# Sums of e over the token groups of batches 0 to 2 on VectorE in a fused cross-attention and ReGLU kernel

## The chip, the cores and the metric

One core of one Trainium2 chip. The metric is the device time of one execution in microseconds (us). The kernel before takes 224.06 us, the median of three runs (224.03 to 224.24).

## The reference

Eight batches b with eight heads; x has 512 tokens of 64 numbers per head, state has 32 rows of 64. The attention runs both ways, and its result goes through a feed-forward layer:

```
scores  = x @ state^T / 8          a  = softmax over the 32 states
xread   = a @ state
scores2 = state @ x^T / 8          a2 = softmax over the 512 tokens
sread   = a2 @ x
h       = concat([xread, sread]) over tokens, heads side by side   -> 4352 rows of 512
out     = (relu(h @ w_gate) * (h @ w_val)) @ w_out                   (512 -> 1536 -> 512)
```

scores2 is scores transposed. So one e = exp(scores) serves both directions: xread divides it by its sums over the states, sread by its sums over the tokens. The change is about the sums over the tokens.

## The kernel before, in words

The 512 tokens of a batch lie as 128 partitions by four groups c (NC = 4), the eight heads as two halves kc (NK = 2) of four heads. e of one batch is the tile e_sn: 128 partitions, kc, c, and 4 heads x 32 states = 128 columns. Four such tiles exist.

The weights are applied through state: U = state @ w (u_unit, c_unit, copied out by u_out L309 and c_out L319), and the normalised a, transposed to ANS, is multiplied with U. gv_mm (L324) makes gate and value products into two PSUM banks, relu (L351, on ACT, the ScalarE) writes g_sb, mult (L355, on DVE, the VectorE) writes h_sb. With 12 blocks of 128 columns (jf) for each batch these are the bulk of the work. The last product with w_out goes by seven block products (o_half, L419, a Strassen-like scheme): POOL (GpSimd) forms sums of h blocks (h_sums, L385 to L387; h_last, L394), and once the sums of w_out blocks (w_sum, L363). Results leave through o_c (L429, ACT copies the w bank), o_a (L435, DVE adds the z bank) and DMAs on SP.

Attention of a batch: att_sc (L186), att_exp (L190, ACT), att_sum (L196, L198, DVE), att_scale (L202, DVE, or POOL where the list says so), then transposes (att_T and att_out L222, or a DMA).

sread of a batch is sr_mm. It first multiplies x (stationary) with e into the bank sr_ps (32 matmuls at L235 for batches 0 to 2, whose x was cast while it was loaded; 16 at L240 for the others). Behind that it sums e over the tokens with sel, a matrix of ones: a matmul with sel sums over the partitions, and the four groups c accumulate in PSUM. Where held has no ("es", b), that is 2 parities x 2 halves x 4 groups = 16 matmuls of 64 columns (L255). Where it has, only 8 (L247): the four groups have been added before by sr_pre (three adds in float32, L263, on POOL), the sum is split into two bfloat16 parts, the high one by an ACT copy (L265) and the rest by a subtraction (sr_low, L271), and the matmuls go over these two parts. The sums es_f and the parts es have one buffer each. sr_norm (L277, L282) divides and writes br. br feeds the products of the sread rows at the end of the kernel.

Order. Nothing is scheduled by a planner at run time. Each engine works off its own instructions in the order in which the program gives them, and waits on semaphores of other engines. For batches 0 to 2, and part of 3 and 4, the order is a list of steps written out by hand (program, L568 to L602), where srm.0 is sr_mm(0), mu.1.8 is mult(1, 8) and so on: ga and gb are the halves kc of gv, re is relu, mu mult, oh o_half, oc and oa o_c and o_a, u and uo u_unit and u_out, sc, ex, nr and nx the attention steps, aT and ao att_T and att_out, hs and hl h_sums and h_last, ws w_sum, xc a cast of x, srm and srn sr_mm and sr_norm. From batch 3's fifth block on, a loop over batches and blocks gives the order (L635 to L660). There sr_pre and sr_low are called for batches 3 to 7 (L647, L648), with POOL. In the list they are not called: batches 0 to 2 take the 16 matmuls of L255. PSUM has six general banks (ps_r) that all products, transposes and scores share; a product waits until the bank it takes has been read out.

Of the kernel before, what the change touches and what calls it, by code (L numbers as in the profile page):

```python
# [11 lines left out]
ALU = mybir.AluOpType  # L12
# [4 lines left out]
def kernel(  # L17
# [9 lines left out]
    nc = tc.nc  # L27

    B, H, S, D = x.shape
# [48 lines left out]
    xf, xb, xT, e_sn, a_sn, ANS, U, hsb, sr_sb = {}, {}, {}, {}, {}, {}, {}, {}, {}  # L78
# [8 lines left out]
    held = {}  # L87
# [168 lines left out]
                                     e[:, kc, c, :, slot(2 * kc, parity)],  # L256
                                     start=False, stop=(parity == 1 and kc == 1 and c == NC - 1), skip_group_check=True)

    def sr_pre(b):

        t = small.tile([128, NK, 128], FP32, name="es_f", tag="es_f", bufs=1)
        for c in range(1, NC):
            nc.gpsimd.tensor_tensor(out=t, in0=t if c > 1 else e_sn[b][:, :, 0], in1=e_sn[b][:, :, c], op=ALU.add)  # L263
        es = held["es", b] = small.tile([128, 2, NK, 128], BF16, name="es", tag="es", bufs=1)
        nc.scalar.copy(out=es[:, 0], in_=t)  # L265
        held["es_f", b] = t

    def sr_low(b, eng="pool"):

# [264 lines left out]
    ws = ((moe_w_gate, wg_sb), (moe_w_val, wv_sb))  # L534
# [23 lines left out]
    def x_cast(b, i, eng):  # L558
# [5 lines left out]
             "gb": lambda b, jf: gv(b, jf, (1,)), "re": relu, "mu": mult, "oh": o_half, "oc": o_c, "oa": o_a, "os": o_s,  # L564
             "hs": h_sums, "hl": h_last, "ws": w_sum, "xd": lambda b: x_dma(b, (nc.sync,)), "xg": lambda b: x_dma(b, (nc.gpsimd,)),
             "xh": x0_cast, "xc": x_cast,
             "xt": x_trans_dma, "aD": att_aT_dma, "srp": sr_pre, "srl": sr_low, "srm": sr_mm, "srn": sr_norm}
    program = """  # L568
    stc.0.2.dve spin.7 stT.0.2 sto.0.2.1.act spin.1 xh.0.dve spin.1 xT.0.0 sto.0.2.0.dve xh.1.act xT.0.1
    xo.0.0.dve xT.0.3 xo.0.1.dve sc.0.0 spin.1 xo.0.3.dve ex.0.0 nr.0.0 nx.0.0 xT.0.2 xo.0.2.act sc.0.1 ex.0.1  # L570
# [12 lines left out]
    mu.0.11 xo.2.3.act ga.0.10 gb.0.10 sc.2.0 re.0.10 mu.0.10 hs.0.1 ga.1.10 gb.1.10 ex.2.0 re.1.10 ws.0.pool  # L583
    ga.1.11 sc.2.1 ex.2.1 u.2.1.0 gb.1.11 nr.2.0 re.1.11 oh.0.1 nx.2.0 uo.2.1.0.0.act mu.1.11 aT.2.0 mu.1.10
    c.1.4 uo.2.1.0.1.act u.2.0.0 ao.2.0.act oh.0.2 oh.0.3 co.1.4.0.dve ga.1.8 nr.2.1 xc.3.0.act ws.1.pool
    hs.0.2 oc.0.1 oh.0.4 co.1.4.1.act xc.3.1.pool uo.2.0.0.0.act nx.2.1.pool ga.1.9 xt.3 oa.0.3 oh.0.6
    ws.2.pool gb.1.8 re.1.8 gb.1.9 oh.0.5 ws.3.pool re.1.9 mu.1.8 aT.2.1 hl.0 uo.2.0.0.1.act xd.4 xc.4.0.pool
    xc.4.1.pool hs.1.0 ao.2.1.act oh.0.7 hs.1.2 ga.2.0 gb.2.0 mu.1.9 ga.2.3 gb.2.3 xt.4 hs.1.1 ga.2.1 gb.2.1
    re.2.0 oc.0.5 mu.2.0 re.2.1 ga.2.2 re.2.3 gb.2.2 re.2.2 mu.2.1 oh.0.8 xd.5 u.2.1.1024 mu.2.3 u.2.0.1024
    uo.2.0.1024.0.dve uo.2.1.1024.0.act uo.2.0.1024.1.act oh.0.9 u.2.1.512 u.2.0.512 oc.0.9 oh.0.10  # L590
    uo.2.0.512.0.act uo.2.1.512.1.act sc.3.0 uo.2.1.512.0.dve ga.2.5 oa.0.9 oh.0.12 oh.0.13 uo.2.1.1024.1.act
    ga.2.4 uo.2.0.512.1.act gb.2.4 oh.0.11 re.2.4 gb.2.5 ga.2.7 oc.0.11 oh.1.0 os.0.11 mu.2.2 ex.3.0 mu.2.4
    oa.0.13 re.2.5 sc.3.1 ga.2.6 mu.2.5 nr.3.0 gb.2.6 srm.0 nx.3.0 ex.3.1 oh.1.1 srn.0 re.2.6 gb.2.7 re.2.7
    mu.2.6 nr.3.1 ga.2.8 mu.2.7 gb.2.8 re.2.8 oh.1.2 mu.2.8 u.3.0.0 uo.3.0.0.0.act u.3.0.512 uo.3.0.512.0.act
    uo.3.0.0.1.act oh.1.3 stT.4.8 u.3.1.0 uo.3.1.0.0.act nx.3.1.pool ga.2.9 aD.3 gb.2.9 sto.4.8.0.act oc.1.1
    oa.1.3 re.2.9 mu.2.9 srm.1 srn.1 sto.4.8.1.act uo.3.0.512.1.act oh.1.4 oh.1.5 oc.1.5 ga.2.10 gb.2.10
    ga.2.11 re.2.10 gb.2.11 mu.2.10 re.2.11 mu.2.11 xc.5.0.act oh.1.6 oh.1.7 u.3.1.512 u.3.1.1024 u.3.0.1024
    oh.1.8 hs.2.0 uo.3.1.0.1.dve ga.3.0 gb.3.0 uo.3.1.512.0.act uo.3.0.1024.0.act xc.5.1.pool sc.4.0 ga.3.1
    oh.1.9 hl.1 uo.3.1.1024.1.dve hs.2.1 uo.3.1.1024.0.act uo.3.1.512.1.act hs.2.2 ex.4.0 ga.3.3 gb.3.1 re.3.0
    ga.3.2 uo.3.0.1024.1.dve re.3.1 gb.3.2 mu.3.0 oc.1.9 oa.1.9 re.3.2 gb.3.3 oh.1.10 re.3.3 xt.5 mu.3.3 srm.2  # L600
# [9 lines left out]
    def at(b, jf, f, *args):  # L610
        units.setdefault(NF * b + jf, []).append(lambda: f(*args))
# [33 lines left out]
            at(s, 3, x_dma, b + 2, (nc.sync,))  # L645
    for b in range(3, B):
        at(*((b, 5) if b < B - 1 else (b, 2)), sr_pre, b)  # L647
        at(*((b, 5) if b < B - 1 else (b, 2)), sr_low, b, "pool")  # L648
        at(*((b + 1, 0) if b < B - 1 else (b, 4)), sr, b)
    for g in range(first, NF * (B + 1)):  # L650
        b, jf = divmod(g, NF)
# [44 lines left out]
```

## Time and profile before

| what | value |
|---|---|
| median of three runs | 224.06 us |
| the profiled execution's own time | 224.17 us |
| its span in the profile | 222.1 us |
| mean granted TensorE clock | 0.997 |
| busy: PE, DVE, ACT, POOL | 213.4, 150.3, 128.7, 164.1 us |
| L255, the 16 sums matmuls of batches 0 to 2 | 48, started from 64.8 to 84.4 us |
| L263, the sums on POOL of batches 3 to 7 | 15, started from 88.9 to 175.3 us |

A row of the timeline gives start (us from the span's start), duration, engine, line, operation, what is written from what, shape, and in brackets the idle time ahead of it with what ended it. Rows of the same kind that follow each other are merged (x6). Durations of neighbours may overlap by some hundredths. PE is TensorE. A row of the stretches gives for each engine the busy us, in brackets the number of instructions started, then granted clock and DMA share.

### The profile page before, as it was taken

To read this page: it belongs to the slowest core of one execution; us is meant where nothing else is said; L and a number is where in the kernel's file an instruction comes from. 1 tells how busy PE (TensorE), PEld (TensorE's weight loads), DVE (VectorE), ACT (ScalarE), POOL (GpSimd) and SP (SyncE) were. 2 spreads that over 40 slices of the span, in tenths; PEclk is the share of its full clock that TensorE was granted. 3 is DMA by queue.
4 is the path that set the end of the run, shared out by engine and by line. 5 is a ranking of instruction groups with operands and counts; after the bars stand their busy time and mean duration, and the time that the engine had idled before them with its cause. 6 is when DMAs were issued, how large, how long until landed. Compare 5 with 4: busy or idle time off the path is not lost.

```text
span 222.1 us, 5525 instructions
## 1 busy us (share of the span) xinstructions
PE 213.4 (96%) x2214; PEld 139.3 (63%) x2214; DVE 150.3 (68%) x263; ACT 128.7 (58%) x247; POOL 164.1 (74%) x162
## 2 busy tenths in 40 slices
PE   6879999999999999999999999999999999999992
PEld 2535445565665657656765666566656666888881
DVE  3579967855486848878787778777977485343531
ACT  2468976876757883566556655656565454322231
POOL 7946199899999996699949993996299719933210
PEclk9999999999999999999999999999999999999998
DMA  6999999039195409920298037102320121021106
GB/s 160 193 196 196 193 201 282 20 62 265 31 206 201 97 0 207 243 72 3 74 233 218 3 91 191 52 0 97 83 61 0 50 97 47 3 96 47 50 27 209
DMA packets 42361, 25.32 MB, mean 114 GB/s; under 512 B 18816, under 2 KB 41856, under 8 KB 42336
## 3 DMA queue, kind: packets, MB, share of 16 engines
q1 hardware_dynamic: 29408, 17.04, 29.4%
q0 software_dynamic: 12416, 7.41, 22.1%
q10 hardware_dynamic: 512, 0.52, 0.7%
q8 instruction: 17, 0.28, 0.5%
q14 instruction: 8, 0.07, 0.1%
HBM read 18.35 MB, written 8.91 MB: 123 GB/s over the span
## 4 chain that ended last, share of the span: by engine, by line
PE 82%; POOL 7%; ACT 4%; DVE 3%; DMA 2%; issue 1%; DVEq 0%; POOLq 0%
PE gv_ps L324 34%; PE w_ps L419 17%; PE z_ps L419 12%; PE gv_ps L342 5%; PE up L299 4%; PE sc_ps L186 2%; DMA st_f<-in_state_dram 2%; POOL s L386 2%; POOL s L385 2%; POOL h_sb L387 2%; POOL h_sb L394 2%; PE zs_ps L419 1%; ACT g_sb L351 1%; PE ws_ps L419 1%; PE xT_ps L169 1%; PE upc L299 1%
## 5 line engine op out<-in xcount | busy, mean ns | idle before, releaser
L355 DVE TENSOR_TENSOR h_sb<-gv_ps,g_sb 128x512 bf16<-128x512 f32 (+1 forms) x108 | 69.1, 657 | 42.3 <-ACT g_sb L351 31.3
L324 PE MATMUL gv_ps<-ans,U 128*128 128x512 bf16 x384 | 94.9, 379 | 0.2
L351 ACT ACTIVATE g_sb<-gv_ps 128x512 bf16<-128x512 f32 (+1 forms) x108 | 61.4, 576 | 37.3 <-PE gv_ps L324 27.5
L419 PEld LDWEIGHTS <-h_sb 128*128 128x128 bf16 x510 | 49.4, 98 | 16.4 <-issue 1.7
L324 PEld LDWEIGHTS <-U 128*128 128x128 bf16 x384 | 35.7, 98 | 31.7 <-issue 1.7
L385 POOL TENSOR_TENSOR s<-h_sb 128x512 bf16<-128x512 bf16 x24 | 27.7, 1153 | 19.3 <-DVE h_sb L355 19.3
L394 POOL TENSOR_TENSOR h_sb<-h_sb,s 128x512 bf16<-128x512 bf16 x24 | 27.0, 1152 | 7.2 <-PE z_ps L419 7.2
L429 ACT COPY o_sb<-w_ps 128x512 f32<-128x512 f32 x32 | 18.8, 587 | 18.4 <-PE w_ps L419 15.8
L386 POOL TENSOR_TENSOR s<-s,h_sb 128x512 bf16<-128x512 bf16 x24 | 28.0, 1167 | 1.9
L309 ACT CAST U<-up 128x512 bf16<-128x512 f32 x43 | 22.7, 595 | 10.0 <-PE up L299 10.0
L387 POOL TENSOR_TENSOR h_sb<-h_sb 128x512 bf16<-128x512 bf16 x24 | 28.1, 1171 | 0.0
L419 PE MATMUL w_ps<-wo_sb,h_sb 128*128 128x256 bf16 x192 | 26.2, 273 | 0.0
L419 PE MATMUL z_ps<-wo_sb,h_sb 128*128 128x256 bf16 x186 | 24.1, 273 | 0.0
L419 PEld LDWEIGHTS <-s 128*128 128x128 bf16 x204 | 19.2, 98 | 7.7 <-issue 2.8
L435 DVE TENSOR_TENSOR o_sb<-z_ps,o_sb 128x512 f32<-128x512 f32 (+1 forms) x23 | 15.5, 675 | 6.8 <-ACT o_sb L429 4.2
L309 DVE CAST U<-up 128x512 bf16<-128x512 f32 x29 | 18.4, 684 | 1.6 <-PE up L299 1.6
L196 DVE TENSOR_REDUCE cs<-e_sn 128x16 f32<-128x512 bf16 x16 | 10.9, 680 | 5.4 <-ACT e_sn L190 5.4
L190 ACT ACTIVATE e_sn<-sc_ps 128x512 bf16<-128x512 f32 x16 | 9.6, 600 | 6.5 <-PE sc_ps L186 6.5
L419 PE MATMUL w_ps<-t2w,s 128*128 128x256 bf16 x96 | 13.0, 273 | 0.0
L419 PE MATMUL w_ps<-t,h_sb 128*128 128x256 bf16 x96 | 12.3, 272 | 0.1
L419 PE MATMUL z_ps<-t,s 128*128 128x256 bf16 x90 | 12.0, 273 | 0.0
L299 PEld LDWEIGHTS <-stT 64*32 64x32 bf16 x480 | 6.1, 89 | 7.1 <-issue 4.6
(86 smaller groups left out, 228.5 us busy)
## 6 DMA issues: line engine op xcount, KB each, us to landing
out_dram<-o_sb SPq DMA_DIRECT2D x31, 256.0 KB, 2.7
xf<-in_x_dram SPq DMA_DIRECT2D x4, 1024.0 KB, 6.9
wg_sb<-in_moe_w_gate_dram POOLq DMA_DIRECT2D x6, 256.0 KB, 9.4
wv_sb<-in_moe_w_val_dram POOLq DMA_DIRECT2D x6, 256.0 KB, 9.8
wo_sb<-in_moe_w_out_dram POOLq DMA_DIRECT2D x2, 768.0 KB, 15.7
xf<-in_x_dram POOLq DMA_DIRECT2D x1, 1024.0 KB, 18.8
xb<-in_x_dram POOLq DMA_DIRECT2D x3, 256.0 KB, 7.0
xb<-in_x_dram POOLq DMA_DIRECT2D x1, 512.0 KB, 11.8
```

Source lines behind the costliest of these rows:

```text
L299: nc.tensor.matmul(dst[kc][q:q + 32], stT[r:r + 64, b, j, 32 * sl:32 * sl + 32], wsb[r:r + 64, j, lo:lo + n], start=True, stop=True)
L309: copy[eng](out=U[b][:, w, kc, lo:lo + 512], in_=held["u", b, w, lo][kc])
L324: nc.tensor.matmul(ps[w], U[b][:, w, kc, f0:f0 + 128], ANS[b][:, kc].rearrange("p c t -> p (c t)"), start=(kc == 0), stop=(kc == NK - 1))
L351: nc.scalar.activation(out=g_sb[:, 0:n], in_=ps[0][:, 0:n], func=AF.Relu)
L355: nc.vector.tensor_tensor(out=dst, in0=ps[1][:, 0:n], in1=held["g", b, jf][:, 0:n], op=ALU.mult)
L385: tt(out=s_block(b, 1, i), in0=a21, in1=a22, op=ALU.add)
L386: tt(out=s_block(b, 2, i), in0=s_block(b, 1, i), in1=a11, op=ALU.subtract)
L387: tt(out=a21, in0=a11, in1=a21, op=ALU.subtract)
L394: {"dve": nc.vector, "pool": nc.gpsimd}[eng].tensor_tensor(out=a12, in0=a12, in1=s_block(b, 2, i), op=ALU.subtract)
L419: nc.tensor.matmul(ps[:, HM * c:HM * c + HM], a[:, i, 128 * c:128 * c + 128], w[:, i], start=(i == 0 and (p in ("p1", "p2", "p5") and c == ...
L429: nc.scalar.copy(out=o_sb, in_=held["acc", b, "w", 0])
L435: nc.vector.tensor_tensor(out=o_sb[:, cols], in0=banks[c if isinstance(c, int) else 0][:, cols], in1=o_sb[:, cols], op=ALU.add)
```

## The change

Batches 0 to 2 get the sums ahead of their sr_mm too, so that sr_mm takes the branch with 8 matmuls. sr_pre gets an engine to add on, and the ACT copy becomes a function of its own, sr_high. In the loop, batches 3 to 7 call the three one after the other, on POOL, ACT and POOL as before. In the list, for each of batches 0 to 2, three steps are new: srp (three adds on DVE), srh (the copy on ACT) and srl (the subtraction, on DVE).

```
-    def sr_pre(b):
+    def sr_pre(b, eng="pool"):

         t = small.tile([128, NK, 128], FP32, name="es_f", tag="es_f", bufs=1)
         for c in range(1, NC):
-            nc.gpsimd.tensor_tensor(out=t, in0=t if c > 1 else e_sn[b][:, :, 0], in1=e_sn[b][:, :, c], op=ALU.add)
+            {"dve": nc.vector, "pool": nc.gpsimd}[eng].tensor_tensor(out=t, in0=t if c > 1 else e_sn[b][:, :, 0],
+                                                                    in1=e_sn[b][:, :, c], op=ALU.add)
+        held["es_f", b] = t
+
+    def sr_high(b):
+
         es = held["es", b] = small.tile([128, 2, NK, 128], BF16, name="es", tag="es", bufs=1)
-        nc.scalar.copy(out=es[:, 0], in_=t)
-        held["es_f", b] = t
+        nc.scalar.copy(out=es[:, 0], in_=held["es_f", b])
...
     for b in range(3, B):
         at(*((b, 5) if b < B - 1 else (b, 2)), sr_pre, b)
+        at(*((b, 5) if b < B - 1 else (b, 2)), sr_high, b)
         at(*((b, 5) if b < B - 1 else (b, 2)), sr_low, b, "pool")
```

The list with the new steps (marked here by brackets, the other steps as before, left out where dots stand):

```
 ... uo.2.0.0.0.act nx.2.1.pool ga.1.9 xt.3 oa.0.3 [srp.0.dve] oh.0.6
 ws.2.pool gb.1.8 re.1.8 gb.1.9 oh.0.5 ws.3.pool re.1.9 mu.1.8 aT.2.1 hl.0 uo.2.0.0.1.act [srh.0] xd.4 xc.4.0.pool
 xc.4.1.pool hs.1.0 ao.2.1.act oh.0.7 hs.1.2 ga.2.0 gb.2.0 mu.1.9 [srl.0.dve] ga.2.3 gb.2.3 ...
 ... os.0.11 mu.2.2 [srp.1.dve] ex.3.0 mu.2.4 oa.0.13 re.2.5 sc.3.1 ga.2.6 mu.2.5 nr.3.0 gb.2.6 srm.0 nx.3.0
 ex.3.1 oh.1.1 srn.0 [srh.1] re.2.6 gb.2.7 re.2.7 mu.2.6 [srl.1.dve] nr.3.1 ga.2.8 mu.2.7 gb.2.8 re.2.8 oh.1.2
 mu.2.8 [srp.2.dve] u.3.0.0 ... oc.1.1 oa.1.3 re.2.9 mu.2.9 srm.1 srn.1 [srh.2] sto.4.8.1.act
 uo.3.0.512.1.act oh.1.4 oh.1.5 oc.1.5 ga.2.10 gb.2.10 ga.2.11 re.2.10 gb.2.11 mu.2.10 [srl.2.dve] re.2.11 mu.2.11 ...
```

More of the change, by code (lines that the diff above doesn't have):

```diff
@@ L566 @@
              "xh": x0_cast, "xc": x_cast,
-             "xt": x_trans_dma, "aD": att_aT_dma, "srp": sr_pre, "srl": sr_low, "srm": sr_mm, "srn": sr_norm}
+             "xt": x_trans_dma, "aD": att_aT_dma, "srp": sr_pre, "srh": sr_high, "srl": sr_low, "srm": sr_mm, "srn": sr_norm}
     program = """
@@ L585 @@
     c.1.4 uo.2.1.0.1.act u.2.0.0 ao.2.0.act oh.0.2 oh.0.3 co.1.4.0.dve ga.1.8 nr.2.1 xc.3.0.act ws.1.pool
-    hs.0.2 oc.0.1 oh.0.4 co.1.4.1.act xc.3.1.pool uo.2.0.0.0.act nx.2.1.pool ga.1.9 xt.3 oa.0.3 oh.0.6
-    ws.2.pool gb.1.8 re.1.8 gb.1.9 oh.0.5 ws.3.pool re.1.9 mu.1.8 aT.2.1 hl.0 uo.2.0.0.1.act xd.4 xc.4.0.pool
-    xc.4.1.pool hs.1.0 ao.2.1.act oh.0.7 hs.1.2 ga.2.0 gb.2.0 mu.1.9 ga.2.3 gb.2.3 xt.4 hs.1.1 ga.2.1 gb.2.1
+    hs.0.2 oc.0.1 oh.0.4 co.1.4.1.act xc.3.1.pool uo.2.0.0.0.act nx.2.1.pool ga.1.9 xt.3 oa.0.3 srp.0.dve oh.0.6
+    ws.2.pool gb.1.8 re.1.8 gb.1.9 oh.0.5 ws.3.pool re.1.9 mu.1.8 aT.2.1 hl.0 uo.2.0.0.1.act srh.0 xd.4 xc.4.0.pool
+    xc.4.1.pool hs.1.0 ao.2.1.act oh.0.7 hs.1.2 ga.2.0 gb.2.0 mu.1.9 srl.0.dve ga.2.3 gb.2.3 xt.4 hs.1.1 ga.2.1 gb.2.1
     re.2.0 oc.0.5 mu.2.0 re.2.1 ga.2.2 re.2.3 gb.2.2 re.2.2 mu.2.1 oh.0.8 xd.5 u.2.1.1024 mu.2.3 u.2.0.1024
@@ L591 @@
     uo.2.0.512.0.act uo.2.1.512.1.act sc.3.0 uo.2.1.512.0.dve ga.2.5 oa.0.9 oh.0.12 oh.0.13 uo.2.1.1024.1.act
-    ga.2.4 uo.2.0.512.1.act gb.2.4 oh.0.11 re.2.4 gb.2.5 ga.2.7 oc.0.11 oh.1.0 os.0.11 mu.2.2 ex.3.0 mu.2.4
-    oa.0.13 re.2.5 sc.3.1 ga.2.6 mu.2.5 nr.3.0 gb.2.6 srm.0 nx.3.0 ex.3.1 oh.1.1 srn.0 re.2.6 gb.2.7 re.2.7
-    mu.2.6 nr.3.1 ga.2.8 mu.2.7 gb.2.8 re.2.8 oh.1.2 mu.2.8 u.3.0.0 uo.3.0.0.0.act u.3.0.512 uo.3.0.512.0.act
+    ga.2.4 uo.2.0.512.1.act gb.2.4 oh.0.11 re.2.4 gb.2.5 ga.2.7 oc.0.11 oh.1.0 os.0.11 mu.2.2 srp.1.dve ex.3.0 mu.2.4
+    oa.0.13 re.2.5 sc.3.1 ga.2.6 mu.2.5 nr.3.0 gb.2.6 srm.0 nx.3.0 ex.3.1 oh.1.1 srn.0 srh.1 re.2.6 gb.2.7 re.2.7
+    mu.2.6 srl.1.dve nr.3.1 ga.2.8 mu.2.7 gb.2.8 re.2.8 oh.1.2 mu.2.8 srp.2.dve u.3.0.0 uo.3.0.0.0.act u.3.0.512 uo.3.0.512.0.act
     uo.3.0.0.1.act oh.1.3 stT.4.8 u.3.1.0 uo.3.1.0.0.act nx.3.1.pool ga.2.9 aD.3 gb.2.9 sto.4.8.0.act oc.1.1
-    oa.1.3 re.2.9 mu.2.9 srm.1 srn.1 sto.4.8.1.act uo.3.0.512.1.act oh.1.4 oh.1.5 oc.1.5 ga.2.10 gb.2.10
-    ga.2.11 re.2.10 gb.2.11 mu.2.10 re.2.11 mu.2.11 xc.5.0.act oh.1.6 oh.1.7 u.3.1.512 u.3.1.1024 u.3.0.1024
+    oa.1.3 re.2.9 mu.2.9 srm.1 srn.1 srh.2 sto.4.8.1.act uo.3.0.512.1.act oh.1.4 oh.1.5 oc.1.5 ga.2.10 gb.2.10
+    ga.2.11 re.2.10 gb.2.11 mu.2.10 srl.2.dve re.2.11 mu.2.11 xc.5.0.act oh.1.6 oh.1.7 u.3.1.512 u.3.1.1024 u.3.0.1024
     oh.1.8 hs.2.0 uo.3.1.0.1.dve ga.3.0 gb.3.0 uo.3.1.512.0.act uo.3.0.1024.0.act xc.5.1.pool sc.4.0 ga.3.1
```

## The prediction

> **What bounds the kernel now.** I read the page first (busy shares, slices, chain), then TensorE's waits, then busy time in stretches of 8 us around the change.
>
> ```profile
> PE 213.4 (96%) x2214; PEld 139.3 (63%) x2214; DVE 150.3 (68%) x263; ACT 128.7 (58%) x247; POOL 164.1 (74%) x162
> PE   6879999999999999999999999999999999999992
> POOL 7946199899999996699949993996299719933210
> PE 82%; POOL 7%; ACT 4%; DVE 3%; DMA 2%; issue 1%; DVEq 0%; POOLq 0%
> ```
> ```profile
> PE warm_ps L554 <- DVE warm L511: 1.2, 1, 1.2
> ```
> ```profile
> 44.00:52.00 8.00, 8.00 (x82) 5.54 (x80) 4.54 (x8) 5.89 (x12) 8.00 (x6) 1.00 0.57 114
> 68.00:76.00 8.00, 8.00 (x118) 5.18 (x118) 5.39 (x11) 6.82 (x15) 7.92 (x8) 1.00 0.49 143
> ```
>
> PE is busy in every slice from the fourth on, is 82% of the chain, and its longest single wait is the 1.2 us before the first matmul. So a microsecond taken off PE in the list of steps is a microsecond off the end, and a microsecond for which PE is made to wait there is one added. The two stretches are where the change acts: PE has 8.00 of 8 us. But so, nearly, has POOL (8.00 and 7.92), while DVE has 4.54 and 5.39. DVE looks like the free place for the sums. Whether it is free beside a POOL that never pauses is what decides.
>
> **What goes: 24 matmuls.**
>
> ```profile
> 51.03 3.62 PE L324 MATMUL gv_ps<-ans,U 128*128 128x512 bf16 x16
> 54.48 0.82 PE L419 MATMUL w_ps<-wo_sb,h_sb 128*128 128x256 bf16 x6
> ...
> 64.15 0.68 PE L235 MATMUL sr_ps<-e_sn,xb 128*64 128x32 bf16 x32
> 64.76 0.64 PE L255 MATMUL sr_ps<-e_sn,sel 128*128 128x64 bf16 x16
> 65.24 0.82 PE L419 MATMUL w_ps<-wo_sb,h_sb 128*128 128x256 bf16 x6
> ```
>
> From start to start the 16 matmuls of L255 take 65.24 - 64.76 = 0.48 us, 0.03 each. Each of the three batches loses 8 of them: 3 x 8 x 0.03 = **0.72 us saved**, all on the path.
>
> **What comes: 12 instructions on DVE, 3 on ACT.** No row of before has such an add on DVE. The nearest are below (L202, 512 elements, 0.69 us; two of L282, 128 elements, 0.59 together, so 0.29 each). Straight between them, 256 elements take 0.42 us; I use that, with 0.29 and 0.69 as ends. By duration alone three adds are 1.3 us a batch.
>
> The price is not the duration. These adds read both operands from SBUF, as L202 does, and DVE's other frequent product (L355) does not (one operand is in PSUM). Look at what happens when L202 meets POOL:
>
> ```profile
> 42.07 1.15 POOL L385 TENSOR_TENSOR s<-h_sb 128x512 bf16<-128x512 bf16 x1 [0.96 <-DVE h_sb L355]
> 43.30 1.48 POOL L386 TENSOR_TENSOR s<-s,h_sb 128x512 bf16<-128x512 bf16 x1
> ```
> ```profile
> 42.91 0.86 DVE L202 TENSOR_TENSOR a_sn<-e_sn,rc 128x512 bf16<-128x512 bf16 x1
> ```
> ```profile
> 63.94 1.16 POOL L386 TENSOR_TENSOR s<-s,h_sb 128x512 bf16<-128x512 bf16 x1
> 65.05 1.60 POOL L387 TENSOR_TENSOR h_sb<-h_sb 128x512 bf16<-128x512 bf16 x1
> ```
> ```profile
> 64.85 0.79 DVE L202 TENSOR_TENSOR a_sn<-e_sn,rc 128x512 bf16<-128x512 bf16 x1
> ...
> 66.54 0.59 DVE L282 TENSOR_TENSOR br<-sr_ps,rr 64x128 bf16<-64x128 f32 x2
> ```
> ```profile
> 109.09 0.67 POOL L263 TENSOR_TENSOR es_f<-e_sn 128x256 f32<-128x256 bf16 x1
> 109.83 1.93 POOL L263 TENSOR_TENSOR es_f<-es_f,e_sn 128x256 f32<-128x256 f32 x2
> ```
> ```profile
> 109.79 0.69 DVE L202 TENSOR_TENSOR a_sn<-e_sn,rc 128x512 bf16<-128x512 bf16 x1
> ```
>
> At 42.91 and 64.85 a POOL operation was already under way: it kept its 1.15 and 1.16, and L202 took 0.86 and 0.79 instead of 0.69. As if L202 had really begun at 43.08 and 64.95, 0.14 and 0.15 before the POOL row ends. The next POOL operation then stretched, to 1.48 and 1.60. At 109.79 DVE came first, kept 0.69, and the POOL pair took 1.93 where two of 0.67 stand for 1.34. Whoever starts first finishes undisturbed, the other stands still until about 0.15 us before the first one's end. Both waits of DVE fell at the tail of a POOL operation, so these rows bound one such wait from 0.10-0.17 us (what was seen) up to the whole of the POOL operation ahead. I take the whole, because the POOL operation that was ahead did not stretch at all.
>
> Now **batch 0** with that. The step srp.0 stands behind oa.0.3 on DVE; srh.0 on ACT stands ahead of ao.2.1; and TensorE's gb.2.0 needs ao.2.1.
>
> ```profile
> 46.73 0.69 DVE L435 TENSOR_TENSOR o_sb<-z_ps,o_sb 128x512 f32<-128x512 f32 x1
> 49.68 0.69 DVE L355 TENSOR_TENSOR h_sb<-gv_ps,g_sb 128x512 bf16<-128x512 f32 x1 [2.26 <-PE gv_ps L324]
> ```
> ```profile
> 46.85 1.04 POOL L202 TENSOR_TENSOR a_sn<-e_sn,rc 128x512 bf16<-128x512 bf16 x1
> 47.85 3.08 POOL L363 TENSOR_TENSOR t<-wo_sb,t2w 128x1536 bf16<-128x1536 bf16 x1
> 50.90 3.09 POOL L363 TENSOR_TENSOR wo_sb<-wo_sb 128x1536 bf16<-128x1536 bf16 x1
> ```
> ```profile
> 50.02 0.59 ACT L309 CAST U<-up 128x512 bf16<-128x512 f32 x1
> 50.58 0.59 ACT L222 COPY ans<-aT_ps 128x512 bf16<-128x512 bf16 x1
> ```
> ```profile
> L265 ACT CAST es<-es_f x5: 397/405/405, 91.1 to 176.0; 128x256 bf16<-128x256 f32 x5
> ```
>
> DVE has 2.26 us idle there, more than three adds. But POOL runs two operations of 3.08 us, and the adds depend on each other, so a waiting POOL operation takes its turn between two of them. Add 1 asks at 47.4, waits for L202 on POOL (ends 47.89, lets go 47.75), runs to 48.17. The first L363 slips to 48.03 and lets go at 50.96. Add 2 runs 50.96 to 51.38; the second L363 starts at 51.24, lets go at 54.17; add 3 runs 54.17 to 54.59. Then srh.0 on ACT (0.405) to 55.04, ao.2.1 (0.59) to about 55.6. gb.2.0 was due at 51.03 + 2 x 0.215 = 51.46 and now starts at 55.65: **+4.2 us** on PE. Behind add 3 on DVE stand mu.1.8, mu.1.9, srl.0, mu.2.0; they are late by less than PE already is.
>
> The Trainium skill ("SBUF — State Buffer", section "Who interferes with whom") states it as a rule: a VectorE instruction with two SBUF inputs and a GpSimd instruction that reads SBUF exclude each other for the whole instruction. The three meetings above agree (0.86, 0.79 and 1.93 us), but none of them lies early in a long operation. By the rule the sum is the one worked out here; by durations alone it would be -0.5 (rival 2).
>
> **Batches 1 and 2**, now 4.2 us later on PE, while POOL lost only about 1 us and works on with data it has.
>
> ```profile
> 58.20 0.68 DVE L355 TENSOR_TENSOR h_sb<-gv_ps,g_sb 128x512 bf16<-128x512 f32 x1
> 61.40 0.69 DVE L355 TENSOR_TENSOR h_sb<-gv_ps,g_sb 128x512 bf16<-128x512 f32 x1 [2.51 <-ACT g_sb L351]
> ...
> 68.65 1.22 DVE L355 TENSOR_TENSOR h_sb<-gv_ps,g_sb 128x512 bf16<-128x512 f32 x2
> 71.90 0.69 DVE L435 TENSOR_TENSOR o_sb<-z_ps,o_sb 128x512 f32<-128x512 f32 x1 [2.02 <-ACT o_sb L429]
> 72.51 0.68 DVE L355 TENSOR_TENSOR h_sb<-gv_ps,g_sb 128x512 bf16<-128x512 f32 x1
> ...
> 76.48 0.68 DVE L309 CAST U<-up 128x512 bf16<-128x512 f32 x1
> ```
> ```profile
> 69.82 0.41 PE L299 MATMUL up<-wv_sb,stT 64*32 64x512 bf16 x8
> 70.16 1.04 PE L324 MATMUL gv_ps<-ans,U 128*128 128x512 bf16 x4
> ...
> 73.53 1.89 PE L324 MATMUL gv_ps<-ans,U 128*128 128x512 bf16 x8
> ...
> 77.10 0.51 PE L299 MATMUL up<-wg_sb,stT 64*32 64x512 bf16 x8
> ```
>
> - srp.1 has 2.51 us of cover and meets operations of 1.15: waits of 0.25, 0.85 and 0.85 and the adds make 3.2 us, 0.7 late, most of it regained before the next PSUM bank is due. srl.1 stands ahead of mu.2.7 and mu.2.8 (68.65 to 69.87) without idle time before them; their banks are due at 69.82 and 70.38. **+0.45** (0 to 1.0).
> - srp.2 has 2.02 us of cover. PE is then 4.2 - 0.24 + 0.45 = 4.4 late, so oa.1.3 is due at 76.3; DVE comes to the adds at about 74.7, and three waits of about 0.9 with the adds make 3.9. oa.1.3 is 2.25 late, and so is mu.2.9 behind it, which frees the bank that ga.2.10 needs at 73.53 + 0.22. mu.2.9 ended at 73.19, so about 0.5 is slack, less what PE is ahead: **+2.0** (0.5 to 2.5).
> - srl.2 stands ahead of mu.2.11 and the copy at 76.48, which ended at 77.16 where the matmuls that want its bank started at 77.10: half a POOL operation of waiting and the 0.42 itself are **+0.9** (0 to 1.2).
> - The other ACT copies cost 0.4 each: srh.1 waits for srm.0 and still ends ahead of what ga.2.8 needs; srh.2 is late with srp.2 and hides behind it. No DMA is added or moved; POOL's and SP's orders are unchanged. What POOL loses is covered, since PE is later still.
>
> **Sum**: 4.2 + 0.45 + 2.0 + 0.9 - 0.72 = +6.8 us, on the profiled execution's own 224.17 (span 222.1 and 2.1 around it); that execution stands 0.11 above the median of 224.06. From the median: **230.9 us**. With the ends of each term: 4.2 - 0.3 for adds of 0.29 gives 3.9 + 0 + 0.5 + 0 - 0.72 = 3.7, 227.8; 4.2 + 0.3 for adds nearer 0.69, with 1.0 + 2.5 + 1.2 - 0.72, gives 8.5, 232.6.
>
> **Rivals.** That the 24 matmuls don't go is none: in the changed program each of the three batches has 8 of them in place of 16.
>
> 1. *Short waits only.* DVE waits 0.10 to 0.17 each time, as seen, and cuts into the long POOL operations. Then srp.0 takes 1.7 of its 2.26 us and is hidden, but POOL stands still for 4 x 0.28 = 1.1 us before the second L363 ends (50.90 + 3.09 = 53.99), and the matmuls at 54.48 read what it writes: 0.6 of waiting. With 0.1 for ao.2.1 and 0.3 later, less 0.72: +0.3, 224.4. For it: both measured waits are short. Against it: a POOL operation ahead was never stretched. Chance 0.08.
> 2. *The other side: no collision.* An add into f32 doesn't meet POOL at all; DVE's idle 2.26, 2.51 and 2.02 take the sums. What is left is 0.1 at ao.2.1 (srh.0 pushes it from 51.17 to 51.55, due 51.46) and 0.1 at the banks near 70: -0.72 + 0.2 = -0.5, **223.5**, faster. It decides if the adds stay near 0.42 back to back beside POOL's L363. Against it: L202 has the same kind of operands and collides. Chance 0.10.
> 3. *A clock that falls in the gap.* The change would make the first wait of PE of over 1.2 us, and in the stretches above the granted clock is 1.00. If PE ran at half for as long as the gap of 4.2 us, 2.1 are added: 233.0. Chance 0.10. The Trainium skill ("TensorE: Matmul & The Clock Gate", section "Part 1: The HAM clock gate") says that the clock is halved after an idle window of about 3.4 us; no run here shows it.
>
> **How the numbers follow.** The forecast has 0.72, from 227.8 to 232.6; rival 3 rides on it (0.10), rival 1 has 0.08, rival 2 0.10. The range 227.2 to 233.4 holds the forecast and rival 3 and leaves out rivals 1 and 2, 0.18. About 0.2% is what a measurement of this kernel can tell from no change, 0.45 us. Rival 2 gives 0.07 faster and 0.03 same; rival 1 0.04 same and 0.04 slower. Faster 0.07, same 0.07, slower 0.86.
>
> **What would show it.** Right: the second and third add on DVE at 48 to 55 us are recorded 2 to 3 us long (or start that late); mu.1.8 starts near 54.5; ACT waits for es_f ahead of ao.2.1; PE waits about 4 us for ans behind ga.2.0; POOL has idle time near 71; three groups of 8 matmuls at the place of L255. Wrong: the adds each near 0.42 and PE without a wait at 51.5 (rival 2), L363 itself stretched (rival 1), PEclk under 1.00 (rival 3), or waits of PE that begin only at batch 2.

## The result, and the profile after

The changed kernel takes **232.51 us** (median of six runs, 230.39 to 232.81) against 224.06 (six runs, 224.00 to 224.26): a ratio of 1.0359, 95% interval 1.0329 to 1.0388, so 8.45 us slower. Forecast were 230.9, in a range of 227.2 to 233.4. The profiled execution took 232.81 us, with a span of 230.7.

The page of the changed kernel: busy shares, TensorE's slices, the granted clock in slices, the chain of work that ended last.

```profile
PE 215.6 (93%) x2159; PEld 140.1 (61%) x2190; DVE 165.2 (72%) x275; ACT 129.7 (56%) x250; POOL 165.6 (72%) x162
PE   6899999993999979999999999999999999999992
PEclk9999999997699999999999999999999999999998
PE 74%; DVE 8%; POOL 7%; ACT 5%; issue 2%; DMA 2%; another core or an unknown queue 1%; DVEq 0%; ACTq 0%; POOLq 0%
```

Three things are new. In the tenth slice (52 to 58 us) PE is busy for only 3 tenths. In the tenth and eleventh the granted clock is 7 and 6 tenths. And DVE, 3% of the chain before, is 8%. PE's busy time rose by 2.2 us although 24 matmuls went, which already hints that some matmuls took longer.

TensorE's waits in the changed kernel (what waited, for whom: us in total, times, longest):

```profile
PE gv_ps L328 <- ACT ans L222: 4.0, 1, 4.0
...
PE gv_ps L328 <- DVE h_sb L359: 0.8, 1, 0.8
...
PE up L303 <- DVE h_sb L359: 0.4, 1, 0.4
```

Its stretches of 8 us. The first one shown holds the gap (PE busy 4.04, clock 0.68); in the last one POOL has lost its load (3.21 of 8):

```profile
52.00:60.00 8.00, 4.04 (x11) 1.46 (x10) 6.04 (x5) 1.96 (x4) 8.00 (x6) 0.68 0.41 130
60.00:68.00 8.00, 7.63 (x80) 4.66 (x80) 5.54 (x9) 5.27 (x10) 7.84 (x8) 0.89 0.82 208
68.00:76.00 8.00, 7.95 (x106) 5.18 (x107) 7.60 (x13) 5.34 (x10) 3.21 (x3) 1.00 0.27 89
```

The chain of batch 0, engine by engine. First DVE (the three adds of each batch, with what stands behind them), then POOL, ACT and PE:

```profile
47.77 0.82 DVE L263 TENSOR_TENSOR es_f<-e_sn 128x256 f32<-128x256 bf16 x1
48.63 6.42 DVE L263 TENSOR_TENSOR es_f<-es_f,e_sn 128x256 f32<-128x256 f32 x2
54.97 1.28 DVE L359 TENSOR_TENSOR h_sb<-gv_ps,g_sb 128x512 bf16<-128x512 f32 x2
...
66.17 0.42 DVE L263 TENSOR_TENSOR es_f<-e_sn 128x256 f32<-128x256 bf16 x1
66.62 2.55 DVE L263 TENSOR_TENSOR es_f<-es_f,e_sn 128x256 f32<-128x256 f32 x2
...
75.05 0.42 DVE L275 TENSOR_TENSOR es<-es_f,es 128x256 bf16<-128x256 f32 x1
...
77.41 0.42 DVE L263 TENSOR_TENSOR es_f<-e_sn 128x256 f32<-128x256 bf16 x1
77.86 2.55 DVE L263 TENSOR_TENSOR es_f<-es_f,e_sn 128x256 f32<-128x256 f32 x2
...
83.81 1.10 DVE L275 TENSOR_TENSOR es<-es_f,es 128x256 bf16<-128x256 f32 x1
```
```profile
48.27 3.26 POOL L367 TENSOR_TENSOR t<-wo_sb,t2w 128x1536 bf16<-128x1536 bf16 x1
51.50 3.26 POOL L367 TENSOR_TENSOR wo_sb<-wo_sb 128x1536 bf16<-128x1536 bf16 x1
...
70.14 1.15 POOL L391 TENSOR_TENSOR h_sb<-h_sb 128x512 bf16<-128x512 bf16 x1
76.49 1.05 POOL L202 TENSOR_TENSOR a_sn<-e_sn,rc 128x512 bf16<-128x512 bf16 x1 [5.20 <-DVE rc L198]
```
```profile
55.08 0.41 ACT L270 CAST es<-es_f 128x256 bf16<-128x256 f32 x1 [4.04 <-DVE es_f L263]
55.39 0.58 ACT L222 COPY ans<-aT_ps 128x512 bf16<-128x512 bf16 x1
```
```profile
51.46 0.59 PE L328 MATMUL gv_ps<-ans,U 128*128 128x512 bf16 x2
56.02 5.28 PE L328 MATMUL gv_ps<-ans,U 128*128 128x512 bf16 x12 [3.96 <-ACT ans L222]
61.51 0.50 PE L328 MATMUL gv_ps<-ans,U 128*128 128x512 bf16 x1 [0.22 <-issue]
61.85 0.82 PE L423 MATMUL w_ps<-wo_sb,h_sb 128*128 128x256 bf16 x6
...
72.13 0.41 PE L247 MATMUL sr_ps<-es,sel 128*128 128x64 bf16 x8
...
81.66 1.67 PE L328 MATMUL gv_ps<-ans,U 128*128 128x512 bf16 x6 [0.83 <-DVE h_sb L359]
...
85.56 0.40 PE L303 MATMUL up<-wg_sb,stT 64*32 64x512 bf16 x4 [0.37 <-DVE h_sb L359]
```

Read it as a relay. The two adds that begin at 48.63 take 6.42 us, about as long as POOL's two operations of L367 (48.27 to 54.76), with which they alternate. ACT, which has to copy es_f ahead of ao.2.1, is idle for 4.04 us until the third add is through; then ans is copied, and at 56.02 PE goes on, after a wait of 3.96 us. That is the mechanism that the prediction describes, to within 0.2 to 0.5 us at each handover, and this execution was 0.43 us late before the first new step (table below). What it did not have is the next row: twelve matmuls that take 5.28 us at 0.44 each, where 16 took 3.62 before.

**The sum, by starts on PE.** The same instruction is looked up in both traces; where the shift changes, time was lost or won.

| landmark on PE | before | after | shift | what lies between |
|---|---|---|---|---|
| transposes aT.2.1 | 50.15 | 50.58 | +0.43 | there from 10 to 14 us on, ahead of the first new step |
| gb.2.0 | 51.46 (worked out: 51.03 + 2 x 0.215) | 56.02 | +4.56 | the wait for ans: +4.13 |
| oh.0.8, behind 14 matmuls | 54.48 | 61.85 | +7.37 | 5.83 instead of 3.02 us: the clock, +2.81 |
| srm.0 | 64.15 | 71.52 | +7.37 | nothing |
| behind srm.0 | 65.24 | 72.38 | +7.14 | 8 matmuls fewer: -0.23 |
| srm.1 | 71.13 | 78.28 | +7.15 | nothing (the banks of mu.2.7, mu.2.8) |
| behind srm.1 | 72.22 | 79.14 | +6.92 | -0.23 |
| behind the gv of 2.10 and 2.11 | 75.26 | 83.17 | +7.91 | mu.2.9 late behind srp.2: +0.99 |
| behind u.3 | 77.54 | 86.49 | +8.95 | the banks behind srl.2: +1.04 |
| behind srm.2 | 84.39 | 93.10 | +8.71 | -0.24 |
| end of the span | 222.1 | 230.7 | +8.6 | nothing more |

0.43 + 4.13 + 2.81 + 0.99 + 1.04 - 0.70 = 8.70, for a span that is 8.6 longer.

### The profile page after: what moved, and what is told of

Read it like the earlier page. It is cut to its first block, busy times and chain, and to the rows that moved or that the text cites. A ratio compares the mean times of both kernels' runs of the same rounds, so it can differ in the third digit from the quotient of the medians.

```text
span 230.7 us, 5461 instructions
## 1 busy us (share of the span) xinstructions
PE 215.6 (93%) x2159; PEld 140.1 (61%) x2190; DVE 165.2 (72%) x275; ACT 129.7 (56%) x250; POOL 165.6 (72%) x162
## 4 chain that ended last, share of the span: by engine, by line
PE 74%; DVE 8%; POOL 7%; ACT 5%; issue 2%; DMA 2%; another core or an unknown queue 1%; DVEq 0%; ACTq 0%; POOLq 0%
PE gv_ps L328 30%; PE w_ps L423 15%; PE z_ps L423 11%; PE gv_ps L346 5%; DVE es_f L263 4%; PE up L303 3%; PE sc_ps L186 2%; DVE h_sb L359 2%; DMA st_f<-in_state_dram 2%; POOL s L390 2%; ACT g_sb L355 1%; POOL s L389 1%; POOL h_sb L391 1%; POOL h_sb L398 1%; PE zs_ps L423 1%
## 5 line engine op out<-in xcount | busy, mean ns | idle before, releaser
L328 PEld LDWEIGHTS <-U 128*128 128x128 bf16 x384 | 36.4, 100 | 38.8 <-issue 10.4
L398 POOL TENSOR_TENSOR h_sb<-h_sb,s 128x512 bf16<-128x512 bf16 x24 | 27.6, 1177 | 7.1 <-PE z_ps L423 7.1
L263 DVE TENSOR_TENSOR es_f<-es_f,e_sn 128x256 f32<-128x256 f32 x6 | 11.4, 1902 | 0.2
```

What stands on the lines that cost most here:

```text
L263: {"dve": nc.vector, "pool": nc.gpsimd}[eng].tensor_tensor(out=t, in0=t if c > 1 else e_sn[b][:, :, 0], in1=e_sn[b][:, :, c], op=ALU.add)
L328: nc.tensor.matmul(ps[w], U[b][:, w, kc, f0:f0 + 128], ANS[b][:, kc].rearrange("p c t -> p (c t)"), start=(kc == 0), stop=(kc == NK - 1))
L398: {"dve": nc.vector, "pool": nc.gpsimd}[eng].tensor_tensor(out=a12, in0=a12, in1=s_block(b, 2, i), op=ALU.subtract)
```

## The experiments

Times are medians; each ratio is against runs of the kernel before on the same chip. The kernel before took 223.55 to 223.90 us there. Lines of the changed kernel's list are given with the moved steps in brackets.

### 1. Only batch 0, only batches 1 and 2

`b0_only` takes srp, srh and srl of batches 1 and 2 out of the list, `b12_only` those of batch 0.

```
b0_only:  -srp.1.dve -srh.1 -srl.1.dve -srp.2.dve -srh.2 -srl.2.dve
b12_only: -srp.0.dve -srh.0 -srl.0.dve
```

> The sums of batch 0 alone by VectorE; batches 1 and 2 as before. Theory (each add waits for the whole POOL operation ahead, and TensorE's clock falls in the gap): the wait of TensorE behind ga.2.0 stays at 4.1 us, the slow clock behind it costs 2.8 again (less where it is shorter), 8 matmuls fewer give 0.24: 224.1 + 4.1 + 2.8 - 0.24 = 230.8, with single runs near 228.7. Rival (the loss is made by the lateness of all three batches together): clearly less than two thirds of the loss, under 229.

> The sums of batches 1 and 2 alone by VectorE; batch 0 as before. Theory: POOL is busy there with operations of 1.15 us, so three adds take about 3.0 us against 2.5 and 2.0 us of idle VectorE, and the subtractions wait up to 1.1 each: 0.5 to 2.5 us of waiting less 0.48, 224.1 to 226.1, most likely 225.3, without a fall of the clock. Rival (adds cost only their 0.42 us): 223.6.

`b0_only`: 229.82 us (228.11 to 230.44), ratio 1.0242 (1.0193 to 1.0290). `b12_only`: 225.79 (225.51 to 225.89), ratio 1.0082 (1.0067 to 1.0097). The first has the wait for ans, 3.97 us, and the clock at 0.50 behind it; the second has neither, its clock is 1.00, and it has the waits of 0.8 (gv on h_sb) and 0.4 us (up on h_sb) that the whole change has. `b0_only` lies 1 us under what was expected, and its four executions run from 228.11 to 230.44. 5.9 and 1.9 us make 7.8 of the 8.45, which agrees with two independent places within this scatter; three quarters of the 7.8 belong to batch 0.

### 2. Is it the clock? Keeping TensorE busy in the gap

`fill_gap` puts 18 matmuls into the bank of ga.2.0 ahead of its own, which overwrite them; nothing is left out. `fill_half` puts 9.

```
+        if (b, jf, kcs) == (2, 0, (0,)):
+            for i in range(18):
+                nc.tensor.matmul(held["gv", b, jf][0][0], U[b][:, 0, 0, 0:128],
+                                 ANS[b][:, 0].rearrange("p c t -> p (c t)"), start=True, stop=True)
```

> The changed kernel with 18 matmuls more ahead of ga.2.0, into the bank that ga.2.0 then starts anew, so that TensorE works for 3.9 of the 4.1 us in which it waits. Theory (the clock falls because TensorE stands still): the clock stays at 1.00, the 14 products behind the gap take 3.0 and not 5.8 us, 232.5 - 2.8 = 229.7, and the times of single runs lie together. Rival (the products behind the gap are slow for their banks or operands): 232.5, clock or no clock.

> As fill_gap, with 9 matmuls in place of 18, so that TensorE stands still for 2.1 us in place of 0.1 and the end of the gap stays where it is. If the clock falls only after a longer standstill (3.4 us by the page that the prediction names), it stays at 1.00 and the time is that of fill_gap, 230.0. If any standstill above the 1.2 us of the kernel before brings it down, part of the 2.8 us comes back: 231 to 232.5.

`fill_gap`: 230.04 us (229.96 to 230.38), ratio 1.0277 (1.0261 to 1.0292). A program with *more* matmuls than the changed kernel is 6.1 us over the kernel before, not 8.45. Its PE rows at the gap, the 18 dummies and then the 16 real ones:

```profile
51.12 4.05 PE L338 MATMUL gv_ps<-ans,U 128*128 128x512 bf16 x18
55.01 3.87 PE L328 MATMUL gv_ps<-ans,U 128*128 128x512 bf16 x16
```

16 matmuls take 3.87 us again, near the 3.62 of the kernel before. The delay of the adds is still there (the two adds take 6.42 us, ACT's copy of ans ends at 55.64), the half clock is not. That shows the clock as a cost of its own, 2.3 us between the medians (which contain executions with and without the full fall) and 2.81 in the trace.

`fill_half`: 230.34 us (228.81 to 231.08), ratio 1.0307 (1.0267 to 1.0346). The median lies between the two times that were expected. A wait of 2.41 us was left, and the clock fell all the same in the profiled execution:

```profile
55.26 4.87 PE L328 MATMUL gv_ps<-ans,U 128*128 128x512 bf16 x14 [2.41 <-ACT ans L222]
```

The stretches of the changed kernel and of `fill_half`, cut at the moments when the clock changed (busy us of PE stand first, the clock third from the end):

```profile
51.53:54.94 3.41, 0.52 (x3) 0.13 (x2) 3.38 (x2) 0.00 (x0) 3.41 (x3) 1.00 0.83 255
54.94:58.35 3.41, 2.33 (x6) 0.86 (x6) 3.10 (x5) 1.96 (x4) 3.41 (x3) 0.50 0.26 90
58.35:61.76 3.41, 3.19 (x8) 1.21 (x8) 1.08 (x2) 1.09 (x3) 3.33 (x5) 0.50 0.03 5
61.76:65.17 3.41, 3.32 (x50) 1.98 (x49) 1.70 (x4) 2.71 (x6) 3.33 (x4) 1.00 1.03 188
```
```profile
52.93:56.34 3.41, 1.08 (x6) 0.49 (x6) 3.41 (x4) 1.56 (x4) 3.41 (x3) 1.00 0.60 207
56.34:59.75 3.41, 3.41 (x10) 1.21 (x9) 1.80 (x4) 1.49 (x3) 3.41 (x5) 0.50 0.01 4
59.75:63.16 3.41, 3.32 (x50) 1.96 (x49) 1.81 (x4) 2.60 (x5) 3.33 (x4) 1.00 0.74 137
```

In `fill_half` the clock fell at 56.34, a full microsecond after PE had gone on (55.26), and was low for 3.41 us. In the changed kernel it fell at 54.94 and was low for 6.82, twice as long. So in these traces the half clock lasts one or two units of 3.41 us, and the stretch ahead of a fall need not be empty: 1.08 of 3.41 us busy was not enough to keep it. In the changed kernel the stretch that began with the rest of the gap (2.33 busy) was followed by another one at half. The Trainium skill ("TensorE: Matmul & The Clock Gate", section "Part 1: The HAM clock gate") has a free-running window of 3413 ns. Its length agrees with these rows; its words "idle window", read as a standstill of 3.4 us, do not, since 2.41 us sufficed.

If the window runs freely, the fall has no fixed distance from the moment at which PE stops. The traces agree: it came 2.0 us after that moment in `b0_only`, 2.9 in the changed kernel, 3.5 in `fill_half`, 4.1 in `reduce_pool_low` and 4.4 in `srh_late` (the last two are below). One program's executions differ as well, which fits but isn't shown to be due to the window alone. Of the changed kernel's six executions four have a mean clock of 0.981 or 0.982 and take 232.5 to 232.8 us; the other two have 0.988 and 0.993 and take 230.4 and 230.6. Of `fill_half`'s four, two have 0.988 and 0.989 (231.1 and 230.8) and two 1.000 (228.8 and 229.9). `fill_gap` has 0.996 to 1.000 in all four, and a spread of 0.4 us.

### 3. Is the price POOL's long operation?

`split_ws` cuts each of the two operations of L363 (ws.2 and ws.3; L367 after) into six of 256 elements. DVE's adds stay as they are.

```
-        ...tensor_tensor(out=out_, in0=in0, in1=in1, op=ALU.subtract)
+        for i in range(HF) if n > 1 else (slice(None),):
+            ...tensor_tensor(out=out_[:, i], in0=in0[:, i], in1=in1[:, i], op=ALU.subtract)
```

> The changed kernel with the last two sums of w_out blocks (L363) each as six operations of 256 elements in place of one of 1536; the same work on POOL in shorter operations. Theory (an add waits for the end of the POOL operation ahead): the two long adds shrink from 3.2 us to about 0.9 each, the wait of TensorE behind ga.2.0 goes, no fall of the clock; POOL loses about 2 us more up to the end of L363, and the matmuls that read it (at 54.5 in the kernel before) wait about 1.4; batches 1 and 2 cost 2.0 as they did: 224.1 + 1.4 + 2.0 - 0.7 = 226.8, between 225.5 and 229. Rival (the adds are long for another reason, their dependence on each other or their types): they stay at 3.2 us, 232.5.

227.08 us (226.51 to 227.40), ratio 1.0139 (1.0120 to 1.0158): 3.2 us over the kernel before instead of 8.45, by a change to POOL alone. DVE in `split_ws`:

```profile
46.48 0.84 DVE L263 TENSOR_TENSOR es_f<-e_sn 128x256 f32<-128x256 bf16 x1
47.35 1.58 DVE L263 TENSOR_TENSOR es_f<-es_f,e_sn 128x256 f32<-128x256 f32 x2
```

Two adds take 1.58 instead of 6.42 us, and PE has no wait for ans. The six short operations beside them take 4.53 us for what was 3.08. Part of that is the cutting itself: the second six, beside which DVE has only the subtraction, take 3.79 for 3.09. PE waits 0.7 us for wo_sb, and 1.4 and 0.8 for h_sb. So an add's wait goes with the length of the POOL operation that it meets.

### 4. Is it the two operands? One reduction in place of three adds

`one_reduce` lets DVE add the four groups in one reduction, whose one input is in SBUF. srl stays a subtraction of two SBUF operands on DVE.

```
+        if eng == "dve":
+            nc.vector.reduce_sum(out=t, in_=e_sn[b].rearrange("p k c m -> p k m c"), axis=AX.X)
-        for c in range(1, NC):
+        for c in range(1, NC) if eng == "pool" else ():
```

> The changed kernel with one reduction on VectorE (one SBUF operand, 1024 elements) in place of the three adds; the subtractions stay there. Theory (two SBUF operands meet POOL, one does not): the reduction takes about 1.2 us (the 512 elements of L196 take 0.68) beside POOL's L363 and leaves that at 3.08; no wait behind ga.2.0, no fall of the clock. srl.0 now meets the second L363 and waits up to 3 us, and mu.2.0 behind it: 0 to 1.5 us. Between 223.5 and 226, most likely 224.8. Rival (VectorE's adds are slowed by anything on POOL): the reduction is stretched too, over 3 us, and 230 or more.

224.99 us (224.47 to 225.74), ratio 1.0063 (1.0036 to 1.0090): 1.2 us are left of the 8.45. DVE and POOL in `one_reduce`:

```profile
47.39 1.91 DVE L263 TENSOR_REDUCE es_f<-e_sn 128x256 f32<-128x1024 bf16 x1
...
51.00 3.34 DVE L277 TENSOR_TENSOR es<-es_f,es 128x256 bf16<-128x256 f32 x1
```
```profile
47.91 3.10 POOL L369 TENSOR_TENSOR t<-wo_sb,t2w 128x1536 bf16<-128x1536 bf16 x1
50.96 3.09 POOL L369 TENSOR_TENSOR wo_sb<-wo_sb 128x1536 bf16<-128x1536 bf16 x1
```

A control and a treatment lie in one trace. The reduction overlaps the first operation of POOL for 1.4 us. POOL's 3.10 is not stretched. The reduction took more than the 1.2 us expected, but its three instances agree (1.91 to 1.94) beside POOL operations of 1.05 to 3.10 us, which speaks against a wait; no run has it beside an idle POOL. The subtraction, with two operands in SBUF, meets the second one and takes 3.34 us; undisturbed, at 75.05 in the changed kernel, it takes 0.42. It makes mu.2.0 late, and PE waits for that:

```profile
54.99 0.81 PE L330 MATMUL gv_ps<-ans,U 128*128 128x512 bf16 x3 [0.94 <-DVE h_sb L361]
```

That is most of what is left of the loss.

### 5. Moving the copy

`srh_late` puts srh.0 behind ao.2.1, so that ACT does not make ans wait for es_f; the adds stay.

```
 ... uo.2.0.0.1.act xd.4 xc.4.0.pool xc.4.1.pool hs.1.0 ao.2.1.act [srh.0] oh.0.7 ...
```

> The changed kernel with the copy srh.0 on ScalarE behind ao.2.1 in place of ahead of it. Theory: TensorE then isn't stopped at gb.2.0 but at ga.2.3, which waits for a bank that mu.1.8 frees, and mu.1.8 stands behind the adds on VectorE (starts at 55.0, ends 55.65): the gap is 3.6 in place of 4.1 us, the clock falls all the same: 231 to 232.5. Rival (ScalarE's queue is the only way in which the adds reach TensorE): the gap goes, 225 to 226.

230.19 us (230.02 to 231.72), ratio 1.0306 (1.0270 to 1.0343). The wait for ans is gone, and another one stands in its place, in PE's row of `srh_late`:

```profile
54.39 4.41 PE L328 MATMUL gv_ps<-ans,U 128*128 128x512 bf16 x12 [3.47 <-DVE h_sb L359]
```

The multiplication mu.1.8 stands behind the adds on DVE and frees the bank that is needed next. Two chains led from the adds to PE, 0.5 us apart; cutting one shows the other. The time is below the 231 to 232.5 expected: the clock fell for one unit in the profiled execution (55.30 to 58.71), while two of the four executions have a mean clock of 1.000.

### 6. A version without the loss

`reduce_pool_low` combines the reduction on DVE with the subtraction on POOL (srl.0 there behind hs.1.0) and srh.0 behind ao.2.1.

> One reduction on VectorE for each batch, the subtractions on POOL (srl.0 behind hs.1.0, srl.1 ahead of nx.3.1, srl.2 ahead of the cast xc.5.1), and srh.0 behind ao.2.1. No instruction is left on VectorE that meets POOL. Theory: the 24 matmuls are saved and nothing is paid on TensorE: 224.06 - 0.72 = 223.3, up to 0.3 more for small waits. Rival (POOL is so full that 2.0 us more of it come out at the end): 224 to 226.

227.38 us (226.49 to 228.16), ratio 1.0160 (1.0127 to 1.0193): a miss. DVE, then PE:

```profile
63.32 1.89 DVE L263 TENSOR_REDUCE es_f<-e_sn 128x256 f32<-128x1024 bf16 x1 [4.53 <-POOL es L277]
```
```profile
65.86 0.31 PE L186 MATMUL sc_ps<-stT,xT 128*128 128x64 bf16 x5 [2.84 <-DVE h_sb L361]
```

es_f has one buffer. The reduction of batch 1 may not write it before the subtraction of batch 0 has read it, and that stood on POOL behind two casts and a group of sums, and began at 62.62. DVE waited 4.53 us, PE 2.84, and the clock fell once more (to 0.50 from 67.2 to 70.6). The expectation looked at the durations and not at the buffer.

`reduce_pool_low2` moves the subtractions forward on POOL: srl.0 right behind hl.0, and so ahead of the two casts xc.4, srl.1 ahead of hs.1.1, which stands behind srh.1 now, and srl.2 ahead of xc.5.1 as before.

> As reduce_pool_low, but srl.0 stands on POOL right behind hl.0, and srl.1 ahead of hs.1.1, so that the one buffer of es_f is free when the next batch's reduction is due; srh.0 behind ao.2.1. Theory (reduce_pool_low lost 2.8 us because srp.1 waited for srl.0, which stood behind hs.1.0 on POOL; beyond that nothing meets POOL): the reductions of 1.9 us fit into 2.26, 2.51 and 2.02 us of idle VectorE, TensorE waits for nothing new, 224.06 - 0.72 = 223.3, up to 0.3 more. Rival (POOL is too full for three subtractions of 0.67): 224.5 or more, with POOL late at hs.2 and hl.1.

223.40 us (222.77 to 224.59) against 223.55 (222.56 to 224.34), ratio 1.0002 (0.9979 to 1.0025). The loss is gone, and the 0.72 us of the matmuls do not show either. The trace of `reduce_pool_low2` has a place where time is given back: ACT, then PE.

```profile
90.92 0.40 ACT L272 CAST es<-es_f 128x256 bf16<-128x256 f32 x1 [3.17 <-POOL es_f L265]
```
```profile
93.33 0.40 PE L305 MATMUL up<-wv_sb,stT 64*32 64x512 bf16 x4 [0.34 <-ACT g_sb L357]
...
94.06 0.40 PE L305 MATMUL up<-wg_sb,stT 64*32 64x512 bf16 x4 [0.32 <-DVE h_sb L361]
```

Batch 3's sums on POOL end at 90.9 us, since POOL has no pause from 73 us on. ACT's copy waits for them for 3.17 us with two relus queued behind it, and PE, which was ahead, waits for banks.

`late_three` therefore calls batch 3's copy and subtraction two blocks later; `late_ctrl` does only that to the kernel before.

```
-        at(*((b, 5) if b < B - 1 else (b, 2)), sr_high, b)
-        at(*((b, 5) if b < B - 1 else (b, 2)), sr_low, b, "pool")
+        at(*((b, 7 if b == 3 else 5) if b < B - 1 else (b, 2)), sr_high, b)
+        at(*((b, 7 if b == 3 else 5) if b < B - 1 else (b, 2)), sr_low, b, "pool")
```

> The variant before it (the reduction on DVE, the subtraction on POOL), with batch 3's ACT copy and subtraction called two blocks later, behind the relus. Theory: in that variant 0.7 to 1.2 us were given back at about 91 us because POOL, now without idle time, came late with batch 3's sums, ACT's copy waited 3.17 us for them, and two relus stood behind the copy; then TensorE waited 0.34 and 0.32 us at the products of U. With the relus ahead of the copy both waits of TensorE go and the start of 88.1 us in the kernel before is kept earlier by 0.65 to 1.2 us to the end: ratio to before 0.995 to 0.997, about 222.5 to 223.0 us on a before of 223.6. Rival: POOL itself is full and late; then the next sums of h are late instead, a wait of TensorE at about 94 to 99 us takes the place of these, and the ratio stays at 1.000 (0.999 to 1.001).

> The kernel before with nothing but that move of batch 3's copy and subtraction two blocks later. Theory and rival alike: TensorE doesn't wait there in the kernel before, so the move alone is worth nothing: ratio 1.000 (0.999 to 1.001), and what late_three gains beyond this is due to the sums.

`late_three`: 223.56 us (222.27 to 224.08) against 223.63 (222.42 to 224.46), ratio 0.9991 (0.9966 to 1.0017). `late_ctrl`: 223.52 (222.66 to 224.11), ratio 0.9987 (0.9967 to 1.0007). In the trace the step did what it should: ACT's copy has no wait,

```profile
90.89 0.41 ACT L272 CAST es<-es_f 128x256 bf16<-128x256 f32 x1
```

and PE none between 85 and 104 us. The time does not tell it apart from the kernel before. Executions of one and the same program scatter by 1.4 to 2.0 us on these two chips. In the profiled executions of `reduce_pool_low2` and `late_three` the scores of the first batch start at 9.10 and 9.11 us, in that of the kernel before at 10.24, long before the list reaches a changed step; of the 1.35 us by which `late_three` is ahead at 102 us, 1.14 are there at 20 us. What remains, 0.2, is there in `late_ctrl` too (0.55 behind at 84 us, 0.35 at 95), so in these traces it comes with the move and not with the sums. That the version gains anything is not shown.

The trace of `late_three` shows where the 0.72 us went this time. Between srm.0 and srm.1 PE loses 0.63 us (1.37 ahead of the kernel before, then 0.74). At 67.41 it waits for h_sb, because DVE is late with an instruction that was there from the start:

```profile
63.71 1.43 DVE L202 TENSOR_TENSOR a_sn<-e_sn,rc 128x512 bf16<-128x512 bf16 x1
```

It has two SBUF operands and begins 0.26 us into a POOL operation (L392, 63.45 to 64.60). In `reduce_pool_low2` the same product begins 0.11 us ahead of that operation, takes 0.69, and PE loses nothing there. So a shift of some tenths of a microsecond decides whether this collision costs as much as the matmuls bring.

## Why the prediction was right in its mechanism and short in its sum

- **Batch 0, the wait: right.** Forecast +4.2, measured +4.13. mu.1.8 was expected near 54.5 and started at 54.97, of which 0.43 is the late start of this execution. Experiments 3 and 4 show the two premises singly: the length of the POOL operation (two adds in 6.42 against 1.58 us) and two SBUF operands (the subtraction stretched from 0.42 to 3.34, the reduction beside POOL not).
- **The clock: the step of the sum that failed.** "A clock that falls in the gap" was a rival at 0.10, priced 2.1 us, and so left out of the sum. It came true in most executions, cost 2.81 us in the profiled one, and is more than the whole difference between 230.9 and 232.5. Its price was wrong in kind too: half of the gap. The half clock is not paid during the gap, when PE does nothing, but behind it, 3.41 us at a time, of which half is lost while PE is busy. 5.83 - 3.02 is what that came to in two units. The ground for the low chance was that no wait in the kernel before was long enough to show it, which is an absence of evidence and not evidence against it.
- **srl.1 and the banks near 70 us: 0 for +0.45.** POOL was idle by then (71.29 to 76.49 us), srl.1 took 0.42 at 75.05, and PE was 7.1 us late, not 4.2.
- **srp.2: +0.99 for +2.0.** The first add of batches 1 and 2 came about 0.1 us before the recorded end of a POOL operation and took 0.42; the two behind it took 2.55 together, 1.27 each. That is 3.0 us instead of 3.9, so the term had one wait too many. PE also came later than assumed, which probably gave slack; no run shows that singly.
- **srl.2: +1.04 for +0.9**, with the subtraction at 1.10 us, most of it waiting.
- **The 24 matmuls: -0.70 for -0.72.** Three groups of 8 stand where the groups of 16 were.
- The errors partly cancel: 2.81 + 0.43 too little, 0.45 + 1.01 too much, the rest small. That 232.5 lies in the range is luck in part. The forecast's own upper end, 232.6, was made of longer adds and longer waits in batches 1 and 2, which did not come; and beyond it the range reached over rival 3, to 233.4.
- **The rivals.** Short waits only: no, POOL's operations took 3.26 us each (3.08 before) while DVE stood still. No collision: no, 6.42 us.

What stays open: the +0.43 of the changed kernel at 10 to 14 us. The eight score matmuls there are recorded with 0.61 us instead of 0.41 at a granted clock of 1.00, ahead of every changed step; other executions start 1.1 us earlier. The profiled execution of `late_ctrl`, which has none of the new steps, has the same 0.61 us and the same 50.58 us for aT.2.1. So it does not come from the change; it is a scatter of the start, whose cause no run here looks at.

## What to carry to other kernels

Look for "idle" time on VectorE beside a busy GpSimd with its operands in mind: an instruction that reads two SBUF operands can cost the whole length of the GpSimd operation that it meets. Here three dependent adds beside two operations of 3.1 us took 7 us and one reduction with a single SBUF input 1.9. Where a change makes TensorE stand still for as long as here (the shortest standstill with a fall was 2.41 us), put the clock into the sum, at half of 3.4 us or of twice that, and not among the rivals. And before work is moved between queues, count the buffers: a single one ties the queues together (4.53 us of DVE here). A saving of tenths of a microsecond on TensorE can be lost at the next collision: the 0.72 us of the matmuls never showed in the time.

## What the runs showed of the hardware beyond that

- A standstill of 2.41 us (`fill_half`) or 2.84 us (`reduce_pool_low`) can halve the granted clock, in some executions of a program and not in others; single waits of 0.94 (`one_reduce`) and 0.83 us did not. The half clock lasted 3.41 or 6.82 us.
- The exclusion is not symmetric in its harm. POOL's operations of 3.08 us lost 0.18 each, the adds between them 2.8 each: an add of 0.42 us that had to wait for a long operation paid nearly all of it, the long one less than the add's own time.
- A reduction over the four groups, whose elements lie 128 apart, takes 1.91 to 1.94 us for 1024 elements, more than three undisturbed adds would (3 x 0.42 = 1.3, an estimate), and was still the better choice next to a busy GpSimd here.
